# Modulation weights in two transfers (16 and 112 partitions), and TensorE's head out of its two-pass loop

## The chip, the cores and the metric

The kernel runs on one core of a Trainium2 chip. A core has five engines that follow their own instruction streams and meet at semaphores: TensorE (PE in the profile; its weight loads stand apart as PEld), VectorE (DVE), ScalarE (ACT), GpSimd (POOL) and SyncE (SP). SyncE computes nothing here: it issues transfers, which 16 DMA engines carry out between the main memory and the on-chip memory of 128 partitions. The metric is the device time of the whole program in microseconds (us), the median of several runs.

## What is computed

A decode step of one conditioned transformer block, for 8 sequences with one new token each. Model width is 512; there are 32 query heads over 8 key/value heads of width 128, and a cache of 8192 positions for each key/value head. All inputs are bf16.

```
mod = silu(c) @ w_mod                        # w_mod 512 x 3072 -> six vectors of 512
sa, ca, ga, sb, cb, gb = the six vectors
h = layernorm(x) * (1 + ca) + sa
q = h @ wq                                   # 512 x 4096: 32 heads of 128
p = softmax(q k^T / sqrt(128))               # k, v: 8 sequences x 8 heads x 8192 x 128
x = x + ga * ((p v) @ wo)
h = layernorm(x) * (1 + cb) + sb
x = x + gb * (relu(h @ w1 + b1)^2 @ w2 + b2)
```

The caches are nearly all of the bytes: 64 units of 4 MB. Weights add `w_mod` (3 MB), `wq` and `wo` (4 MB each), `w1` and `w2`.

## The kernel before

The work has three stages. The **head** computes the modulation vectors, the normalised input and the queries. The **loop** runs 8 passes, one for each sequence: a pass takes four key units (transposes on TensorE, copies out of its accumulators by VectorE and ScalarE, then scores), a softmax, and four value units. The **post** part does the last value unit of the last sequence, the output projection and the feed-forward block.

Transfers. SyncE issues all large loads in one order written by hand: the modulation weights (line 293), `wq` (line 295), then cache units, with two small biases and `wo` (lines 456 to 458) between the second and the third unit. Key and value units go round a ring of four buffers of 128 partitions by 32 KB (`RING`). Before it issues the load of unit n+4 (line 372), SyncE waits until TensorE has finished with unit n. The first loads borrow ring buffers: the modulation weights lie in buffer 2 (24 KB in each partition) and `wq` in buffer 3, so the third and fourth key unit wait for the matmuls that read those. ScalarE issues two small loads, `c` (line 291) and `x` (line 292), at the same time. At the end SyncE loads the last value unit in four pieces (line 367) and the feed-forward weights (lines 664 and 666).

Head on TensorE, in this order: transposes of silu(c) (line 380) and of x (line 386), transposes of the normalised x (line 399), the modulation product (line 405, its first matmul waits for the semaphore `d_wm` of the modulation weights), small matmuls that turn its result (lines 419 and 428), the query product (line 405 again, after `wq`), and the turn of that (line 438). Then the loop begins with the transposes of the first key unit (line 486).

## Time and profile before

| | |
|---|---|
| median of 3 runs | 669.52 us (669.29 to 670.03) |
| the profiled execution, device time | 669.29 us |
| its span, first to last instruction | 667.5 us |
| bytes moved | 283.85 MB, 425 GB/s over the span |
| TensorE busy | 515.8 us (77%) |
| VectorE busy | 302.4 us (45%) |
| ScalarE busy | 258.9 us (39%) |
| mean granted TensorE clock | 0.893 of full speed |

The span is the time between the first and the last instruction on the profiler's record; 1.8 us of the device time lie around it. In the page, a line of 40 digits gives the busy share of 40 equal slices in tenths. Lines of the transfer queues give packets, megabytes, and the time that the packets took as a share of 16 DMA engines over the stretch asked for; a packet is counted in the stretch in which it starts. q1 is the queue that SyncE issues to, q10 ScalarE's, and q8 and q14 carry instructions. In a timeline, a line begins with start and length in us, the engine (SPq is SyncE's issue queue) and the line of the kernel; what stands in brackets is the idle time before it and what ended it.

### The profile page before, as it was taken

The numbers are of one execution on the slowest core, as the hardware profiler recorded it, in microseconds if no ns is written. First come the engines' busy times: TensorE is split into PE (matmuls) and PEld (weight loads), VectorE is DVE, ScalarE is ACT, GpSimd is POOL, SyncE is SP. The second block draws the span as 40 slices with busy tenths as digits, with TensorE's granted clock in tenths as the row PEclk, the third lists the DMA queues.
The fourth block names the chain that finished last, engine by engine and source line by source line (L and its number), as shares of the span: only waits on it lengthen the run. The fifth ranks groups of instructions, "written<-read, shape, count | busy, mean of one in ns | idle before, by whom it ended". The sixth has DMA issues, their size and how long they took to land.

```text
span 667.5 us, 15496 instructions
## 1 busy us (share of the span) xinstructions
PE 515.8 (77%) x7064; PEld 345.8 (52%) x7064; DVE 302.4 (45%) x571; ACT 258.9 (39%) x289; POOL 18.6 (3%) x76
## 2 busy tenths in 40 slices
PE   3494975899739975699748987499856998389886
PEld 1383731775328742477317753287425773177534
DVE  1262741466216751367315662166513673156622
ACT  2161640466206650266404661056602664046610
POOL 7300000000000000000000000000000000000000
PEclk9697997799959998799977999599985999789996
DMA  9999999999999999999999999999999999999996
GB/s 373 438 408 437 430 421 435 436 428 428 436 436 428 428 436 436 428 426 436 438 426 426 438 438 424 428 438 438 420 432 438 434 422 434 438 434 422 434 417 265
DMA packets 12176, 283.85 MB, mean 425 GB/s; under 512 B 1250, under 2 KB 1283, under 8 KB 3588
## 3 DMA queue, kind: packets, MB, share of 16 engines
q1 hardware_dynamic: 12116, 283.65, 99.1%
q8 instruction: 9, 0.15, 0.1%
q10 hardware_dynamic: 48, 0.02, 0.0%
q14 instruction: 3, 0.02, 0.0%
HBM read 283.66 MB, written 0.01 MB: 425 GB/s over the span
## 4 chain that ended last, share of the span: by engine, by line
PE 52%; DMA 36%; ACT 7%; DVE 2%; SPq 2%; issue 1%
PE PS L486 36%; DMA ring<-in_A_k_cache_dram 32%; PE PS L503 9%; ACT P_sb L569 5%; PE PS L623 2%; DMA ring<-in_B_w_dram 2%; DMA ring<-in_A_wq_dram 2%; SPq L666 1%; PE PS L476 1%; ACT KTb L491 1%; DVE O_sb L633 1%; PE PS L470 1%; PE PS L581 1%; DVE Pm L595 1%; PE PS L601 0%
## 5 line engine op out<-in xcount | busy, mean ns | idle before, releaser
L491 ACT ACTIVATE KTb<-PS 128x1024 bf16<-128x1024 bf16 x192 | 196.7, 1024 | 330.8 <-PE PS L486 330.8
L486 PE MATMUL PS<-IDENT,ring 128*128 128x128 bf16 x4096 | 268.1, 228 | 50.0 <-DMA ring<-in_A_k_cache_dram 50.0
L486 PEld LDWEIGHTS PS<-IDENT,ring 128*128 128x128 bf16 x4096 | 247.5, 103 | 98.8 <-DMA ring<-in_A_k_cache_dram 51.2
L493 DVE COPY KTb<-PS 128x1024 bf16<-128x1024 bf16 x320 | 209.9, 687 | 144.4 <-PE PS L486 142.2
L623 PE MATMUL PS<-ring,Pm 128*32 128x512 bf16 x992 | 70.4, 434 | 46.2 <-DMA ring<-in_A_v_cache_dram 45.3
L503 PE MATMUL PS<-KTb,Qb 128*32 128x512 bf16 x1024 | 79.2, 386 | 4.5 <-ACT KTb L491 4.5
L633 DVE CAST O_sb<-PS 128x512 bf16<-128x512 f32 x31 | 21.4, 692 | 126.1 <-PE PS L623 126.1
L623 PEld LDWEIGHTS PS<-ring,Pm 128*32 128x32 bf16 x992 | 26.9, 106 | 84.8 <-DMA ring<-in_A_v_cache_dram 53.0
L569 ACT ACTIVATE P_sb<-PS,negm 128x1024 bf16<-128x1024 f32 x32 | 35.2, 1113 | 20.2 <-DVE negm L564 20.2
L476 PE MATMUL PS<-ONES 128*128 128x512 f32 x80 | 42.1, 630 | 0.0
L581 PE MATMUL PS<-IDENT,P_sb 128*128 128x128 bf16 x256 | 19.8, 220 | 15.4 <-ACT P_sb L569 15.4
L595 DVE COPY Pm<-PS 64x512 bf16<-64x512 bf16 x48 | 20.2, 421 | 25.1 <-PE PS L581 24.6
L581 PEld LDWEIGHTS PS<-IDENT,P_sb 128*128 128x128 bf16 x256 | 14.4, 98 | 25.2 <-ACT P_sb L569 25.2
L470 PE MATMUL PS<-IDENT 128*128 128x512 bf16 x88 | 26.9, 380 | 0.0
L503 PEld LDWEIGHTS PS<-KTb,Qb 128*32 128x32 bf16 x1024 | 15.4, 94 | 21.1 <-ACT KTb L491 8.5
L510 DVE TENSOR_REDUCE m<-PS 128x1 f32<-128x512 f32 x32 | 22.0, 689 | 6.6 <-PE PS L503 6.6
L637 PEld LDWEIGHTS PS<-SEL,O_sb 128*128 128x128 bf16 x124 | 5.8, 98 | 30.5 <-DVE O_sb L633 30.5
L476 PEld LDWEIGHTS PS<-ONES 128*128 128x128 f32 x80 | 12.7, 190 | 10.6 <-issue 10.6
L637 PE MATMUL PS<-SEL,O_sb 128*128 128x8 bf16 x124 | 7.9, 169 | 12.4 <-DVE O_sb L633 12.0
L648 DVE TENSOR_TENSOR oTn<-PS,rinv 128x8 f32 x31 | 6.0, 194 | 14.9 <-PE PS L637 14.9
L470 PEld LDWEIGHTS PS<-IDENT 128*128 128x128 bf16 x88 | 7.7, 105 | 9.1 <-issue 7.2
L491 ACT ACT_TABLE_LOAD x8 | 10.3, 1283 | 3.2 <-issue 3.2
(132 smaller groups left out, 117.0 us busy)
## 6 DMA issues: line engine op xcount, KB each, us to landing
ring<-in_A_k_cache_dram SPq DMA_DIRECT2D x32, 4096.0 KB, 34.2
ring<-in_A_v_cache_dram SPq DMA_DIRECT2D x31, 4096.0 KB, 27.8
ring<-in_A_wq_dram SPq DMA_DIRECT2D x1, 4096.0 KB, 20.2
wo_sb<-in_A_wo_dram SPq DMA_DIRECT2D x1, 4096.0 KB, 47.5
ring<-in_w_mod_dram SPq DMA_DIRECT2D x1, 3072.0 KB, 11.0
ring<-in_A_v_cache_dram SPq DMA_DIRECT2D x1, 2048.0 KB, 23.4
ring<-in_B_w_dram SPq DMA_DIRECT2D x3, 512.0 KB, 20.1
ring<-in_B_w_dram SPq DMA_DIRECT2D x1, 1344.0 KB, 18.7
```

Source lines behind the costliest of these rows:

```text
L470: ts = [op("tensor", lambda e: e.matmul(bank(at).rearrange("p (a r) -> p a r", a=4), IDENT[:, :], rhs)) for _ in range(n)]
L476: ts = [op("tensor", lambda e: e.matmul(bank(at).rearrange("p (a r) -> p a r", a=4), ONES[:, :], rhs)) for _ in range(n)]
L486: t = op("tensor", lambda e, j=j, i=i: e.matmul(STG[j][:, i, :], src[:, 32 * k + 8 * j + i, :], IDENT[:, :], is_transpose=True), [loaded[n ...
L491: stg_free[j] = op("scalar", lambda e, j=j, dst=dst: e.activation(dst, STG[j], ACT.Copy), [t])
L493: stg_free[j] = op("vector", lambda e, j=j, dst=dst: e.tensor_copy(dst, STG[j]), [t])
L503: t = op("tensor", lambda e, hf=hf, q=q, rhs=rhs: e.matmul(PS[32 * q:32 * (q + 1), k, :], Qb[:, 2 * p + hf, :], rhs, start=(p == 0 and hf ...
L510: return op("vector", lambda e: e.tensor_reduce(m4[:, k:k + 1], bank(k), AX.X, ALU.max), [t])
L569: exps.append(op("scalar", lambda e, k=k: e.activation(P_sb[:, k, :, :, :], bank(k).rearrange("p (i x) -> p i x", i=8).unsqueeze(2).to_bro ...
L581: t = op("tensor", lambda e, k=k, i=i: e.matmul(STG[k][:, i, :], P_sb[:, k, i, :, :].rearrange("p h x -> p (h x)"), IDENT[:, :], is_transp ...
L595: done.append(op("vector", lambda e, dst=dst, frm=frm: e.tensor_copy(dst, frm), [t, k_pm]))
L623: t = op("tensor", lambda e, p=p, m=m, cg=cg, vt=vt, Obank=Obank: e.matmul(Obank[32 * cg:32 * (cg + 1), :], lhs[:, p, 32 * m:32 * m + 32], ...
L633: t = op("vector", lambda e, osb=osb, Obank=Obank: e.tensor_copy(osb, Obank), [t])
```

## The change

Two edits. The modulation weights are loaded by two transfers on the same queue and the same semaphore, one into partitions 0 to 15 and one into partitions 16 to 127, where one went into all 128; a wait for them now stands for both. And the loop of two passes around TensorE's head is gone: the head is emitted once, straight through, as on the other engines, and the loop over the sequences begins at place 0 of its fetch block.

```diff
     def _looped(self, e, eng, passes):
         nc, per, pe = self.nc, self.per[e], self.LOOP[e]
         seen, first = {}, {}
-        if e == "tensor":
-            with nc.Fori(0, 2, engines=[pe]) as i:
-                with eng.If(0 < i):
-                    for o in self._part(e, None):
-                        self._emit(eng, o, self._want(e, o, 0), seen)
-                eng.addr_align(bass.FETCH_BLOCK_INSTRUCTIONS, offset=0, max_nops=0)
-        else:
-            for o in self._part(e, None):
-                self._emit(eng, o, self._want(e, o, 0), seen)
+        for o in self._part(e, None):
+            self._emit(eng, o, self._want(e, o, 0), seen)
...
-        with nc.Fori(0, passes, engines=[pe], head_slot={pe: 16} if e == "tensor" else None) as i:
+        with nc.Fori(0, passes, engines=[pe], head_slot={pe: 0} if e == "tensor" else None) as i:
...
-        d_wm = dma("sync", s_wm, lambda e: e.dma_start(
-            RING[:, 2, 0:KT * NMOD], w_mod.rearrange("(p k) n -> p (k n)", k=KT)))
+        wmod_p = w_mod.rearrange("(p k) n -> p (k n)", k=KT)
+        for a, z in ((0, 16), (16, 128)):
+            d_wm = dma("sync", s_wm, lambda e, a=a, z=z: e.dma_start(
+                RING[a:z, 2, 0:KT * NMOD], wmod_p[a:z]))
```

The order of all other instructions is the same on every engine. SyncE issues one transfer more.

## The prediction

> **What bounds the kernel now.** I read the page's slices and queues first.

> ```profile
> PE   3494975899739975699748987499856998389886
> DMA  9999999999999999999999999999999999999996
> q1 hardware_dynamic: 12116, 283.65, 99.1%
> ```

> SyncE's queue q1 keeps the 16 DMA engines busy for 99.1% of the span, in every slice but the last, while PE has gaps in most. Is the queue ever near empty? The view of the line that issues cache units tells:

> ```profile
> L372 SPq DMA_DIRECT2D ring<-in_A_k_cache_dram x32: 327/328/20989, 1.7 to 580.7; - x32
> DMA to landing us min/median/max: 23.2/28.3/46.1
> ```

> A unit is 4.19 MB, which at the 425 GB/s of the page takes 9.9 us; yet none landed less than 23.2 us after its issue. At least 13 us of other transfers always stood ahead of it. So the end is set by the time at which the engines start, the bytes, the rate, and what follows the last landing. An edit to compute costs nothing until it delays an issue by more than those 13 us; a transfer that occupies its DMA engines longer costs its whole excess, because nothing behind it can catch up.

> Next, the start: SyncE's timeline, then q1 in the stretches 1 to 2, 2 to 3, 3 to 4, 4 to 5 and 7 to 8 us (packets, MB, share of 16 engines).

> ```profile
> 0.81 0.39 SPq L293 DMA_DIRECT2D ring<-in_w_mod_dram  x1
> 1.26 0.42 SPq L295 DMA_DIRECT2D ring<-in_A_wq_dram  x1
> 15.48 20.99 SPq L372 DMA_DIRECT2D ring<-in_A_k_cache_dram  x1
> ```

> ```profile
> q1 hardware_dynamic: 7, 0.17, 74.3%
> q1 hardware_dynamic: 9, 0.22, 84.2%
> q1 hardware_dynamic: 14, 0.34, 81.0%
> q1 hardware_dynamic: 16, 0.39, 97.7%
> q1 hardware_dynamic: 17, 0.42, 99.8%
> ```

> 16 packets are 0.39 MB, 24 KB each: one partition's row of the modulation weights, 128 in all, 8 for each DMA engine. A packet's time is share x 16 us / packets: 1.70 us in the first stretch, 1.50 in the second (these 16 are each engine's first), then 0.93, 0.98 and 0.94. The first round thus takes (7 x 1.70 + 9 x 1.50) / 16 = 1.59 us where a later one takes 0.94 (I use the 7 to 8 us stretch): an excess of 0.65 us. The row tells that such packets can take that much longer, not why.

> **Part 1, TensorE's head loop: 0.0 us.** The branches show what it does.

> ```profile
> L131 PEldq COMPARE_BRANCH  x2: 77/154/232, 1.1 to 2.3; - x2
> L134 PEldq COMPARE_BRANCH  x2: 169/236/304, 1.4 to 25.9; - x2
> q8 instruction: 1, 0.02, 6.0%
> q8 instruction: 1, 0.02, 6.9%
> 4.52 0.29 PE L380 MATMUL PS<-IDENT,KTb 8*128 8x8 bf16 x4 [4.52 <-DVE KTb L376]
> 11.83 3.60 PE L405 MATMUL PS<-ring,KTb 128*32 128x512 bf16 x24 [0.66 <-DMA ring<-in_w_mod_dram]
> 31.26 6.19 PE L486 MATMUL PS<-IDENT,ring 128*128 128x128 bf16 x64 [5.04 <-DMA ring<-in_A_k_cache_dram]
> ```

> The empty pass jumps to the loop's fetch block at 1.4 us and is back at 2.3; the head can begin some 1.2 us sooner without it (2.3 - 1.1). But its first matmul waits at 4.52 for VectorE, the later ones for x and weights, so the gain is hidden. The first q8 line (stretch 6 to 7 us) is one 16 KB instruction block, 0.06 x 16 = 0.96 us on one engine. No block comes earlier, so the target of the jump was there already; this one is the block after it. Without the empty pass it is asked for when TensorE enters the loop, after 25.9 us. From 1.4 it took until between 7 and 8 us: up to 6.5 us. Asked for at 26 it is there by 32.5. The next q8 packet starts in the stretch 42 to 43 us; if a block is asked for when TensorE enters the one before it, as I read both rows, TensorE enters the block in question a few us ahead of 42, since it waits for its first key unit until 31.26 and transposes from then on. That is the cover; without it TensorE would stand up to 6.5 us, which the 13 us of queued transfers hide in turn. The bytes are the same. Place 0 in place of 16 moves each block's edge by 16 instructions, some 8 transposes with their weight loads; 64 take 6.19 us, so under 1 us, inside the same cover.

> **Part 2, the added issue: 0.0 us.** One more issue costs SyncE about 0.4 us (0.39 for L293), and `wq`, two key units, the biases and `wo` go out that much later. The engines work on the modulation weights until about 10 us, so nothing runs dry. The wait before L405 now ends with the later transfer. Behind it on TensorE stand the turns, the query product and, through buffer 2, the issue of the third key unit. That issue began at 15.48 and took 20.99 us to get out, so some us of lateness there vanish.

> **Part 3, the shape of the two transfers: +4.6 us.** The bytes are unchanged, as are 8 rows for each engine if both counts divide over 16 engines (16 is 1 x 16, 112 is 7 x 16). What changes is which rows run at the same time, and which engine has which. Before, every large load ran over 128 partitions in one pattern; the trace shows no transfer of 16 or 112, so I bound it. From below: every row takes 0.94 us wherever it goes, 0.0; if the short first transfer also cures the slow first round, -0.65. From above: the 16 rows of the first transfer follow one another, 16 x 0.94 = 15.0 us in place of 1.6, +13.4. Between them I go by the nearest row, the only 24 KB packets that ran slow, the first round: its excess stands already for one round of eight, and I let the other seven, all in the new arrangement, pay it too: 7 x 0.65 = +4.6.

> [...]

> **Sum.** 0.0 + 0.0 + 4.6 on the profiled execution's own 669.29 us gives 673.9. The median shown is 0.23 higher, inside the runs' spread, so I leave that out.

> **The rivals.**

> - *Not slower: the split heals the start.* Rows cost 0.94 us in any partition, and the short first transfer makes the first round as quick: 669.29 - 0.65 = 668.6. For it: the engines' first packets do start uneven (7 before 2 us, 9 after) and slow. Against: that excess may come of a cold start that a split doesn't touch. It decides if 24 KB packets of the first transfer take under 1.59 us. With 0.0 instead, the kernel stays at 669.3.
> - *Rows collide far worse.* If the other rounds pay two such excesses each, 14 x 0.65 = 9.1: 678.4; in full series +13.4, 682.7. For it: 16 engines into 16 neighbouring partitions is what no load did before. Against: even the first round, slow for whatever reason, took below twice 0.94.
> - *The instruction block comes late.* If the loop's own first or second block has to be fetched on demand, TensorE stands up to 6.5 us at its beginning; were the queue not deep, 675.8. Against: 23.2 us from issue to landing at the least.
> - *The change does not do what it says.* If 112 rows don't spread over all 16 engines, 7 rounds become more; 14 engines of 8 rows would be 9 rounds in all against 8, +0.9, 670.2.

> **How the numbers follow.** Forecast 0.53, its own range 672 to 677. Split heals or costs nothing 0.22 (of it 0.08 below 668.2 by a further cure of the engines' unevenness). Worse collision 0.12. Late block 0.05. Uneven spread 0.08, half of it within 0.2%. Against the median 669.52, 0.2% is 1.3 us, about what a measurement of this kernel can tell from no change: slower from 670.9, faster under 668.2. So slower 0.53 + 0.12 + 0.05 + 0.04 = 0.74; same 0.14 + 0.04 = 0.18; faster 0.08. The range goes from 668.7 (the healed start at the median's level) to 678.5 (two excesses), with some 0.2 outside.

> **What would show it.** Right: in the first 5 us q1 packets of 24 KB well over 1.6 us, the first modulation matmul some 4 to 5 us after 11.83, the first key transposes as late after 31.26, all later landings shifted as much, and the DMA line still full. The q8 block moves to 26 to 33 us, with no gap of TensorE near 40. Wrong: shifts under 1 us at 31.26 (part 3 is nothing), or a shift at 31.26 that the end doesn't keep (the DMA engines were not the bound), or an equal start and a later end (something in the loop, blocks first).

## The result, and the profile after

The changed kernel takes 675.67 us (675.12 to 675.97, 4 runs) against 669.61 us (669.29 to 670.03, 4 runs) for the kernel before: 6.06 us more, a ratio of 1.0089 with a 95% interval of 1.0072 to 1.0107. The profiled execution took 675.12 us with a span of 673.3 us, so the span grew by 5.8 us. The forecast of 673.9 had the direction and most of the size.

First the rates by slice of the kernel before, then the page of the changed kernel: its slices, the totals of its transfers and its queues.

```profile
GB/s 373 438 408 437 430 421 435 436 428 428 436 436 428 428 436 436 428 426 436 438 426 426 438 438 424 428 438 438 420 432 438 434 422 434 438 434 422 434 417 265
```

```profile
PE   0684986699839986599756998399856998489886
DMA  9999999999999999999999999999999999999996
GB/s 233 425 414 434 433 424 433 434 434 432 424 434 432 430 436 432 432 430 428 432 430 436 432 434 432 426 432 428 436 432 434 432 426 432 430 434 432 434 413 265
DMA packets 12192, 283.85 MB, mean 422 GB/s; under 512 B 1266, under 2 KB 1299, under 8 KB 3604
q1 hardware_dynamic: 12132, 283.65, 99.1%
q8 instruction: 9, 0.15, 0.1%
```

The megabytes are those of before and the DMA engines are as full (99.1% on q1). But the first slice, 16.8 us long, moved 233 GB/s where it moved 373 before; from the second slice on, the rates are about those of before (425, 414, 434 against 438, 408, 437). The engines were occupied and moved less. q1 has 12132 packets against 12116: 16 more, and the packets under 512 B grew by the same 16 (1250 before). In the trace 16 packets of four bytes end every large load; I read them as the report of each DMA engine, and by that reading both transfers ran on all 16 engines.

Now q1 of the changed kernel in the stretches 1 to 2, 2 to 3, 3 to 6, 6 to 8, 8 to 10 and 10 to 12 us (packets, MB, share of 16 engines).

```profile
q1 hardware_dynamic: 9, 0.22, 122.7%
q1 hardware_dynamic: 7, 0.17, 107.7%
q1 hardware_dynamic: 32, 0.39, 72.7%
q1 hardware_dynamic: 25, 0.61, 118.7%
q1 hardware_dynamic: 22, 0.54, 89.4%
q1 hardware_dynamic: 25, 0.61, 109.5%
```

Read as in the prediction, the 16 packets of the first transfer took (9 x 2.18 + 7 x 2.46) / 16 = 2.30 us each. In the third stretch 16 of the 32 packets are end reports, of about 0.03 us each; with these counted in, the 16 rows took 0.727 x 48 / 16 = 2.18 us. In the next three stretches a packet took 1.52, 1.30 and 1.40 us. Before, it was 1.59 in the first round and 0.94 later.

The timeline of TensorE in the changed kernel: the modulation product, the first key transposes, and the last matmuls; under it the last matmuls before.

```profile
17.03 3.60 PE L400 MATMUL PS<-ring,KTb 128*32 128x512 bf16 x24 [4.61 <-DMA ring<-in_w_mod_dram]
36.45 6.30 PE L481 MATMUL PS<-IDENT,ring 128*128 128x128 bf16 x64 [5.03 <-DMA ring<-in_A_k_cache_dram]
670.56 0.38 PE L761 MATMUL PS<-IDENT,KTb 128*8 128x128 bf16 x4 [0.28 <-DVE KTb L756]
```

```profile
664.73 0.38 PE L766 MATMUL PS<-IDENT,KTb 128*8 128x128 bf16 x4 [0.28 <-DVE KTb L761]
```

They stood at 11.83, 31.26 and 664.73 before: 5.20, 5.19 and 5.83 us later. What was lost by the time the modulation weights are there is still lost at the end.

### The profile page after: what moved, and what is told of

The parts are those of the page before. It is cut to its first block, busy times and chain, and to the rows that moved or that the text cites. A ratio compares the mean times of both kernels' runs of the same rounds, so it can differ in the third digit from the quotient of the medians.

```text
span 673.3 us, 15486 instructions
## 1 busy us (share of the span) xinstructions
PE 517.4 (77%) x7064; PEld 347.1 (52%) x7064; DVE 302.5 (45%) x571; ACT 258.9 (38%) x289; POOL 18.6 (3%) x76
## 2 busy tenths in 40 slices
DMA  9999999999999999999999999999999999999996
## 3 DMA queue, kind: packets, MB, share of 16 engines
q1 hardware_dynamic: 12132, 283.65, 99.1%
## 4 chain that ended last, share of the span: by engine, by line
PE 52%; DMA 37%; ACT 7%; DVE 2%; SPq 1%; issue 1%
PE PS L481 36%; DMA ring<-in_A_k_cache_dram 32%; PE PS L498 9%; ACT P_sb L564 5%; DMA ring<-in_A_wq_dram 3%; DMA ring<-in_B_w_dram 2%; PE PS L618 2%; PE PS L471 1%; ACT KTb L486 1%; SPq L661 1%; DVE O_sb L628 1%; PE PS L465 1%; PE PS L576 1%; DVE Pm L590 0%; PE PS L596 0%
## 5 line engine op out<-in xcount | busy, mean ns | idle before, releaser
L486 ACT ACTIVATE KTb<-PS 128x1024 bf16<-128x1024 bf16 x192 | 196.7, 1024 | 331.2 <-PE PS L481 331.2
L400 PE MATMUL PS<-ring,KTb 128*32 128x512 bf16 x56 | 7.2, 626 | 7.8 <-DMA ring<-in_w_mod_dram 4.6
```

Source lines behind the costliest of these rows:

```text
L486: stg_free[j] = op("scalar", lambda e, j=j, dst=dst: e.activation(dst, STG[j], ACT.Copy), [t])
```

## The experiments

Three theories were set against each other: A, the cost lies in which partitions the 16 DMA engines write at the same time; B, it lies in the number of transfers; C, it lies in the head loop's removal. D came later: the engines run dry behind a short first transfer. All runs start from the kernel before. They were measured in three sets, each on one chip and beside the kernel before (669.44, 669.42 and 669.46 us), and the differences below are taken against these.

**Each part of the change alone: the split.**

```diff
-        d_wm = dma("sync", s_wm, lambda e: e.dma_start(
-            RING[:, 2, 0:KT * NMOD], w_mod.rearrange("(p k) n -> p (k n)", k=KT)))
+        wmod_p = w_mod.rearrange("(p k) n -> p (k n)", k=KT)
+        for a, z in ((0, 16), (16, 128)):
+            d_wm = dma("sync", s_wm, lambda e, a=a, z=z: e.dma_start(
+                RING[a:z, 2, 0:KT * NMOD], wmod_p[a:z]))
```

> The kernel before with the modulation weights in two transfers (16 and 112 partitions) and nothing else; TensorE's two-pass head loop stays. Theory A (placement: the cost comes from which partitions the 16 DMA engines write at the same time) and theory B (count: the cost comes from having one transfer more, whatever its shape) both expect the whole of the change's cost: about +6.0 us, 675.6, with the first modulation matmul near 17.0 us. Theory C (the head loop's removal costs something, by instruction blocks fetched late) expects less by its share; if C is all, 669.6.

Measured: 675.78 us, +6.34, ratio 1.0092 (1.0077 to 1.0108). That is all of the change's cost. The first modulation matmul was expected near 17.0 us and stood at 18.68 in the profiled execution; this line and its last matmuls are

```profile
18.68 3.27 PE L407 MATMUL PS<-ring,KTb 128*32 128x512 bf16 x24 [3.28 <-DMA ring<-in_w_mod_dram]
671.40 0.38 PE L768 MATMUL PS<-IDENT,KTb 128*8 128x128 bf16 x4 [0.28 <-DVE KTb L763]
```

6.85 and 6.67 us later than in the kernel before. Here the whole loss is there by the modulation product, and the end keeps it.

**Each part alone: the head loop removed.**

```diff
-        if e == "tensor":
-            with nc.Fori(0, 2, engines=[pe]) as i:
...
+        for o in self._part(e, None):
+            self._emit(eng, o, self._want(e, o, 0), seen)
...
-        with nc.Fori(0, passes, engines=[pe], head_slot={pe: 16} if e == "tensor" else None) as i:
+        with nc.Fori(0, passes, engines=[pe], head_slot={pe: 0} if e == "tensor" else None) as i:
```

> The kernel before without TensorE's two-pass head loop (the loop over the sequences at place 0 of its block), the modulation weights in one transfer. Theories A and B: 669.6, within 0.7 us (0.1%), the first modulation matmul near 11.8 us and the block that was fetched at 6 us asked for only after TensorE enters the loop at 27 us. Theory C: later by its share, up to 675.6.

Measured: 669.47 us, +0.03, ratio 1.0001 (0.9991 to 1.0010). Theory C falls. The lines are from this kernel: TensorE's entry into the loop over the sequences (first start 27.1 us), the instruction block's packet in the stretch 31 to 32 us, and the timeline's first key transposes.

```profile
L140 PEldq COMPARE_BRANCH  x9: 76/208/315, 27.1 to 647.4; - x9
q8 instruction: 1, 0.02, 6.5%
30.88 6.10 PE L479 MATMUL PS<-IDENT,ring 128*128 128x128 bf16 x64 [5.05 <-DMA ring<-in_A_k_cache_dram]
```

The block that was fetched between 6 and 8 us comes between 31 and 33 (as I read it, while TensorE works on the block before it); the 64 transposes take 6.10 us (6.19 before), so no stall shows in them.

**Number of transfers against their shape.** Two transfers over all 128 partitions, each with half of every row:

```diff
-        d_wm = dma("sync", s_wm, lambda e: e.dma_start(
-            RING[:, 2, 0:KT * NMOD], w_mod.rearrange("(p k) n -> p (k n)", k=KT)))
+        wmod_p = w_mod.rearrange("(p k) n -> p (k n)", k=KT)
+        CW = KT * NMOD // 2
+        for j in range(2):
+            d_wm = dma("sync", s_wm, lambda e, j=j: e.dma_start(
+                RING[:, 2, j * CW:(j + 1) * CW], wmod_p[:, j * CW:(j + 1) * CW]))
```

> The kernel before with the modulation weights in two transfers that both run over all 128 partitions, each half of every row (12 KB). Theory A: no cost beyond the added issue, 669.3 to 670.3, first modulation matmul near 11.8 to 12.3 us. Theory B: as the split, 675.6.

Measured: 669.71 us, +0.27, ratio 1.0004 (0.9995 to 1.0013). And two transfers of 64 partitions, by the loop of the split over `((0, 64), (64, 128))`:

> The kernel before with the modulation weights in two transfers of 64 partitions each (0 to 63, 64 to 127). Theory B: as the split by 16 and 112, 675.6 within 0.7 us, for the count is the same. Theory A: a cost of its own size, since each transfer brings all 16 engines to half of the partitions; no row of this case prices it, more than 1 us away from the split in either direction would speak for A. [...]

Measured: 677.38 us, +7.94, ratio 1.0115 (1.0099 to 1.0130). With the same count of two transfers the cost is 0.3, 6.3 or 7.9 us, as the partitions go. The halves stand 1.6 us above the split, past the 1 us that would speak for theory A.

**The same with eight transfers.** Of 16 partitions each, by the loop of the split over `[(16 * i, 16 * i + 16) for i in range(8)]`:

> The kernel before with the modulation weights in eight transfers of 16 neighbouring partitions. Theory A: every round brings all 16 engines into 16 neighbouring partitions, as only the first round of the changed kernel did, where 24 KB packets took 2.30 us (9 with 122.7% and 7 with 107.7% of 16 engines in the first two stretches of one us). Eight such rounds are 18.4 us against 1.59 + 7 x 0.94 = 8.2 before: +10.2 at the least, 679.8 or more, as the packets of the first round did not meet a full queue yet. Theory B: seven transfers more; the added cost grows with their number, as in the column run of the same count. [...]

Of all 128 partitions each, by the column loop with `CW = KT * NMOD // 8`:

> The kernel before with the modulation weights in eight transfers over all 128 partitions, 3 KB of each row. It has the count of the run with eight transfers of 16 partitions, and the regular pattern of all other loads. Theory A: up to about +1 us (packets of 3 KB in place of 24, and seven issues more of 0.4 us each on SyncE, which the queue hides), 669.6 to 670.6. Theory B: the same time as eight transfers of 16 partitions.

Measured: 687.49 us, +18.07, ratio 1.0269 (1.0253 to 1.0285) by partitions, and 670.01 us, +0.59, ratio 1.0008 (0.9999 to 1.0017) by columns. The modulation product in their timelines, by partitions first:

```profile
29.94 3.60 PE L407 MATMUL PS<-ring,KTb 128*32 128x512 bf16 x24 [15.71 <-DMA ring<-in_w_mod_dram]
```

```profile
12.62 3.18 PE L408 MATMUL PS<-ring,KTb 128*32 128x512 bf16 x24 [2.53 <-DMA ring<-in_w_mod_dram]
```

18.1 us and 0.8 us later than 11.83. Theory B falls. Theory A's floor from the trace was +10.2, well under the 18.07 measured. The floor took each round at the 2.30 us of a first round. By partitions the stretch 12 to 15 us holds 16 rows and 16 end reports:

```profile
q1 hardware_dynamic: 32, 0.39, 111.1%
```

That is 1.111 x 48 / 16 = 3.3 us for a row: once the load was under way, a row into neighbouring partitions took three and a half times the 0.94, where a first round shows two and a half times.

**The short transfer first, or gaps.** The loop of the split over `((0, 112), (112, 128))`:

> The kernel before with the modulation weights in two transfers, the large one first: partitions 0 to 111, then 112 to 127. Theory D (gap: the cost comes from the DMA engines running dry behind a short first transfer, until the second is issued) expects none, 669.5 to 670. Theory A expects most of the cost to stay, since the same shapes are written: the first round has 16 engines on rows 7 apart, the last one on 16 neighbours: 672 to 675.6.

Measured: 676.74 us, +7.28, ratio 1.0114 (1.0097 to 1.0131). Theory D falls: with nothing short in front, the cost is not less. It is also more than the 675.6 that I had given theory A as its upper end; why this order costs a little more is open.

**The price of each shape by itself.** A copy of rows is loaded ahead of the untouched single transfer, into the buffer that `wo` fills later:

```diff
...
+        d_ex = dma("sync", s_ex, lambda e: e.dma_start(wo_sb[:, :, :].rearrange("p h n -> p (h n)")[0:16, 0:KT * NMOD], wmod_p[0:16]))
...
-            A_wo.rearrange("(g p j) n -> p g (j n)", g=8, p=128)))
+            A_wo.rearrange("(g p j) n -> p g (j n)", g=8, p=128)), [d_ex])
```

16 rows into partitions 0 to 15, and the same 16 rows into every seventh partition (`[0:106:7]`):

> The kernel before with one transfer more, ahead of the modulation weights: their first 16 rows once again, into partitions 0 to 15 of the buffer that holds wo later (wo's issue waits for it). It measures the disputed cost by itself: one round of 16 rows, 393 KB more. The bytes alone cost 0.94 us for each engine. Theory A: well over that, as 16 engines write 16 neighbouring partitions: at least the 2.30 us that the first round of the changed kernel took, less the slow first round of 1.59 that it takes over, plus a regular round of 0.94: +1.6 or more, 671.2 or more, and above the run with spread partitions by 1 us or more. Theory B: the same as the run with spread partitions.

> As the run with an extra transfer into partitions 0 to 15, but into every seventh partition (0, 7, ... 105): same bytes, same count of packets, same source rows, same issue. Theory A: nearer to the 0.94 us of the bytes alone, +0.3 to +1.6 (669.9 to 671.2), below the run with neighbouring partitions by 1 us or more. Theory B: the same as that run.

112 rows into partitions 16 to 127 (`[16:128]` from `wmod_p[16:128]`), and as a control all 128:

> The kernel before with one transfer more ahead of the modulation weights: their rows 16 to 127 once again, into partitions 16 to 127 of wo's buffer. It prices the second transfer of the change alone. Its bytes are 7 regular rounds of 0.94 us, 6.6 us: 676.0, and that is what a theory expects by which the 16 neighbouring partitions make all of the cost. Theory A with a cost in both shapes: the 16-row run paid 2.7 - 0.94 = 1.8 us beyond its bytes, so of the split's 6.3 some 4.5 are left for the 112 rows: 680.5 (679 to 681.5).

> Control: the kernel before with all 128 rows of the modulation weights loaded once more into wo's buffer, ahead of the real load, in the regular pattern. Theory A: the bytes alone, 8 rounds of 0.91 to 0.94 us: +7.3 to +7.5, 676.7 to 676.9, and so below the run that adds only 112 rows. A theory by which any added transfer at the start costs more than its bytes expects more.

| added ahead | us | more | ratio (95% interval) | bytes' share | beyond bytes |
|---|---|---|---|---|---|
| 128 rows | 676.63 | 7.17 | 1.0107 (1.0091 to 1.0124) | 7.17 | 0 |
| 16 rows, every seventh partition | 671.17 | 1.75 | 1.0025 (1.0016 to 1.0035) | 0.90 | 0.85 |
| 16 rows, partitions 0 to 15 | 672.14 | 2.72 | 1.0037 (1.0023 to 1.0051) | 0.90 | 1.8 |
| 112 rows, partitions 16 to 127 | 679.84 | 10.38 | 1.0156 (1.0139 to 1.0173) | 6.27 | 4.1 |

The bytes' share is taken from the control: 7.17 / 8 = 0.90 for each round of 16 rows. 112 rows cost 3.2 us more than 128. Neighbouring partitions cost 0.97 us more than spread ones, a little less than the 1 us that theory A had asked for, and the spread rows' +1.75 lies above its +0.3 to +1.6. The first transfer's 1.8 and the second's 4.1 make 5.9 of the split's 6.3 us. The control's 7.17 is a little under the 7.3 that was expected.

The packets show a larger difference than the times. The 16 rows by sevenths all started in the stretch 2 to 3 us; of the neighbours 8 started in 1 to 2 and 8 in 2 to 3:

```profile
q1 hardware_dynamic: 16, 0.39, 132.2%
```

```profile
q1 hardware_dynamic: 8, 0.20, 105.3%
q1 hardware_dynamic: 8, 0.20, 125.0%
```

1.322 x 16 / 16 = 1.32 us for a packet against (1.053 + 1.250) x 16 / 16 = 2.30. The spread packets were not slow at all beside the 1.59 of the first round before. They started late: no packet of q1 started before 2 us, and SyncE came to the issue of `wq` only after 2 us, where with the neighbours it came to it before. So part of the 0.85 us that the spread rows cost beyond their bytes is a late start and not slow packets.

Both runs read the same 16 rows, so for these it is the partitions written that decide. No run does the same for the 112 rows or the halves: a cut by partitions also changes which rows of the weights are read at the same time, and the trace does not tell which engine moves which row. Whether the 112 rows are slow for where they are written or for how they are read is therefore open.

## Why the prediction was right, and where it was off

**What bounds the kernel** held. 5.2 us lost before 17 us are 5.8 us at the end of the same execution, and the control with 128 rows more costs their bytes (7.17 us for 8 rounds, 0.90 each). Where the 0.6 us between 5.2 and 5.8 arose is open; in the run with the split alone nothing was added after the modulation product (6.85, then 6.67).

**Part 1, 0.0 us**, measured +0.03. If the block was asked for when TensorE entered the loop, at 27.1 us, it was there about 33 us, inside the 6.5 us that I allowed. In the changed kernel it was later than the forecast's 26 to 33: its packet starts between 36 and 37 us, since the head was itself 5.2 us late and TensorE entered the loop at 32.5. I had not moved my own window along.

**Part 2, 0.0 us**, holds within what two transfers by columns cost (+0.27). But the lateness of the third key unit's issue did not vanish as I wrote:

```profile
20.68 21.89 SPq L367 DMA_DIRECT2D ring<-in_A_k_cache_dram  x1
```

It began 5.2 us later than at 15.48 and took no less (20.99 before); as I read it, the queue that it waits for was late too. No cost of it shows beside part 3.

**Part 3, +4.6 us**, has the right cause, slower packets under the new arrangement, and a term too small. The single rounds of the changed kernel were 2.30, 2.18 and, taking 1.45 for each of the six others (between the 1.52 and 1.30 above), 8.7 us: 13.2 in all against 1.59 + 7 x 0.94 = 8.2, so +5.0, and 5.2 by TensorE's wait; with what came after, 6.06. I had let seven rounds pay 0.65 each. The measured excess was uneven, 0.7 in the first round, 1.2 in the second and 0.5 in each of the rest.

The row that I sized it by was the wrong one in kind. I took the slow first round of before as a sample of what a bad arrangement costs. The kernel with two transfers by columns shows that it is not; the stretches 1 to 2, 2 to 3 and 4 to 5 us:

```profile
q1 hardware_dynamic: 8, 0.10, 60.2%
q1 hardware_dynamic: 9, 0.11, 46.3%
q1 hardware_dynamic: 32, 0.39, 97.6%
```

Its 12 KB packets took 1.20 and 0.82 us first and 0.49 later, in the regular pattern. So the slow first round belongs to the start: it comes in the regular pattern too, once. Why it is slow no run shows. That 0.65 times seven came near is partly chance. (The range's lower end, 669.52 - 0.65, is 668.9 and not 668.7; nothing rests on it.)

**Why neighbouring partitions cost more** no run shows. For 16 rows the runs show that the partitions written decide (2.30 us for a packet into neighbours, 1.32 into every seventh), not what in the chip makes it so. Nor is the cost one figure: the packets of the changed kernel's first transfer took 0.7 us longer than the first round before (2.30 against 1.59), the added transfer cost 1.8 us beyond its bytes, and with eight such transfers in a row a packet took 3.3 us. Every run that cuts the load by partitions was slower than the one transfer over all 128: +6.34, +7.94, +18.07 and +7.28 us.

**The rivals.** "The split heals the start": the first transfer's packets took 2.30 us, over the 1.59 from which that rival would have decided. "Rows collide far worse": not in this split, but eight transfers of 16 partitions did it (+18.07). "The instruction block comes late": +0.03. "Uneven spread": 16 end reports for each of the two transfers, so by my reading of them all engines took part.

## What to carry to other kernels

In this kernel, bound by its transfers from the first microseconds, a load that made the DMA engines slower cost its excess in full at the end, though it stood first of all (5.20 us at the modulation product, 5.83 at the last matmuls). Where transfers are the bound, look for such a loss at the start. Cut such a load by columns (here two pieces +0.27 us, eight +0.59) and keep all 128 partitions in each piece, for cuts by partitions cost 6.3 to 18.1 us for the same 3 MB. And a busy share near 100% (99.1% on q1 in both kernels) told here that the DMA engines were occupied, not how many bytes they moved (373 GB/s in the first slice before, 233 after): look at GB/s by slice, and at packet times by stretch.

## What was not expected

The prediction did not foresee that a transfer of 112 partitions takes longer than one of 128: added ahead, 10.38 us against 7.17, with an eighth fewer bytes. Nor that rows into neighbouring partitions get slower still once the load is under way (3.3 us against 2.30 in the first round). And the empty first pass of TensorE's head loop buys nothing in this kernel: without it the time is 669.47 us beside 669.44. None of the kernels beat the one before.
